# Two batches in nine-token rows: q, k and v loaded by head halves, kv in two row parts, the first factor by Sqrt, the last columns at full width

## The chip, the core and the metric

The kernel runs on one core of a Trainium2 chip. Its engines are TensorE (PE, matrix products), VectorE (DVE), ScalarE (ACT), GpSimd (POOL) and SyncE (SP, which here only issues transfers). Each has an instruction stream of its own; they meet through semaphores. The metric is the device time of one execution in microseconds (us), lower is better. The times given are medians over runs.

## The reference

q, k and v are fp32 arrays of 8 batches x 8 heads x 576 tokens x 64. An attention without softmax feeds a gated feed-forward layer:

```python
kv  = einsum('bhsd,bhse->bhde', k, v)                 # 64x64 for each batch and head
out = einsum('bhsd,bhde->bhse', q, kv)
out = out / sqrt(mean(out*out, -1) + 1e-6) * g_norm   # per head
x   = out.transpose(0, 2, 1, 3).reshape(4608, 512)    # heads side by side
xn  = x / sqrt(mean(x*x, -1) + 1e-6) * rms_g
y   = (silu(xn @ w_gate) * (xn @ w_val)) @ w_out      # 512 -> 1536 -> 512, fp32 out
```

## The kernel before

**Tiling.** The feed-forward layer makes nine groups of 512 tokens: one for each batch (its first 512 rows) and a ninth, `xr`, that gathers the 64 remaining rows of all eight batches. A group's x is held with features on partitions, in four feature blocks of 128. For each of 12 hidden blocks j, `slots_a` makes a gate product (four matmuls in `mm1`, L609, then Silu on ACT, L620) and a val product (four more, then the product `h` on VectorE, L626). `slots_b` multiplies h by w_out (`mm2`, L631) for each of four token tiles; ACT copies the tile to `osb` (L647) and SP's queue stores it (L649). Batch 0 uses `slots_b_by_j` instead, in which all four output tiles are open at once and their four stores come together at the end.

**Attention.** In a 512-row main part, row p*4+c sits on partition p, chunk c (NC = 4 chunks); the last 64 rows (`rem`) are loaded apart. `kv_mm` forms kv for two heads at once in a 128x128 product (L269), of which only the two diagonal 64x64 blocks are copied out; batch 1 uses 64-wide pieces instead (L263), and batch 0 `kv_pairs` (L281), two head pairs at a time. q is transposed on PE in batches 0 and 1 (`qT_mm`, L301, copied out at L311), by transfers on SP's queue in the others (`qT_dma`, L315 and L317). `o_mm` and `o_pairs` form q kv. The norms need two sums over each head, of out squared and of out squared times g_norm squared. Batches 0 and 1 get them from PE: `oT_mm` forms out transposed, ACT squares it (`sqT_`, L370), a matmul by the selector `sel` sums it (L378, L388). Later batches square on ACT (`sq_`, L348), multiply on GpSimd (`wsq`, L394) and sum on VectorE (`red`, L399). `chain` (L416 to L434) turns both sums into one factor `al`, by twelve small VectorE instructions that end in two Newton steps of 1/sqrt; `xna_` or `xna_pairs` (L444, L341) multiplies. x is then transposed by PE in batches 0 and 1 (`xT_mm`, L465, copied by ACT at L475 and by VectorE at L477, which also apply `gain`), by transfers on SP's queue in the others (`x_dma`, L496).

**Order.** Everything is issued in program order, by hand. Ahead of the loop, batch 0's first two chunks go through the whole attention while spins (`spin`, L227: matmuls on a tile of zeros) occupy PE. k and q arrive in fp32 through SP's and ACT's queues (`load_main`, L174) and are cast (L196); v arrives through GpSimd's queue, whose transfers cast to bf16 (`load_v01`). Then come 24 slots (`early`): gate and val of all 12 hidden blocks on the first 256 tokens; behind them `behind(n)` carries on with batch 0's other two chunks. From there a `Placer` takes over: it holds all later slots in order, knows how much time each engine has to spare in each kind of slot (`ROOM`) and how far it may fall behind (`BEHIND`), and puts the attention of the next batches between them. `place_second` places batch 1 by fixed slots, `place_attention` the others. `place_casts` puts the casts of staged q, k, v on GpSimd. `load_all(b)` issues a batch's loads on SP's queue while the batch two before it is in its feed-forward part: `load_all(3)` is placed six slots into batch 1, behind batch 2's `qT_dma`. Some loads carry an added wait (`add_manual_dep`) on an earlier transfer: batch 1's q on the last gate weights, batch 2's on the last of w_out.

`rows_of` gives the rows to which an output tile is stored: one store of 128 rows, or two of 64 in the group of the remaining rows.

Of the kernel before, what the change touches and what calls it, by code (L numbers as in the profile page):

```python
# [86 lines left out]
def kernel(  # L87
# [23 lines left out]
    FB0 = [sum(FB[:n]) for n in range(len(FB))]  # L111
    where = [(n, j - FB0[n]) for n in range(len(FB)) for j in range(FB0[n], FB0[n] + FB[n])]
# [28 lines left out]
    v01 = consts.tile([128, H, (NC + 1) * D], BF16, name="v01")  # L141
    k1 = consts.tile([128, H, (NC + 1) * D], BF16, name="k1")
# [11 lines left out]
    for t in range(2):  # L154
        nc.vector.memset(rems[t][0][REM:], 0.0)
    nc.vector.memset(v01[REM:, :, MAIN // 128 * D :], 0.0)
    idle = consts.tile([128, MAIN], BF16, name="idle")
    nc.vector.memset(idle, 0.0)
    nc.vector.memset(kvs[0], 0.0)
    nc.vector.memset(sel, 0.0)  # L160
    for half in range(2):
        nc.vector.memset(sel[half * D : (half + 1) * D, 0, half : half + 1], 1.0)

# [5 lines left out]
    def load_main(b, t, heads=(0, H), cs=(0, NC), queue=nc.sync):  # L169
        if (b, t) not in staged:  # L170
            staged[b, t] = stage.tile([128, H, NC * D], FP32, name="stg")
        h0, h1 = heads
        view = src[t][b, :, 0:MAIN, :].rearrange("h (p c) d -> p h (c d)", c=NC)
        return queue.dma_start(  # L174
            out=staged[b, t][:, h0:h1, cs[0] * D : cs[1] * D], in_=view[:, h0:h1, cs[0] * D : cs[1] * D]
        )

    def load_v01(b, heads=None, t=2):
        to = v01 if t == 2 else k1
        if heads is None:  # L180
            return nc.gpsimd.dma_start(
                out=to[:REM, :, NC * D :], in_=src[t][b, :, MAIN:S, :].rearrange("h p d -> p h d")
            )
        view = src[t][b, :, 0:MAIN, :].rearrange("h (p c) d -> p h (c d)", c=NC)[:, heads[0] : heads[1]]
        return nc.gpsimd.dma_start(out=to[:, heads[0] : heads[1], : NC * D], in_=view)
# [5 lines left out]
    def cast_main(b, t, eng, heads=(0, H), cs=(0, NC)):  # L191
        if (b, t) not in mains:
            mains[b, t] = qkv.tile([128, NC, H, D], BF16, name=f"main_{'qkv'[t]}")
        h0, h1 = heads
        copy = eng.copy if eng is nc.scalar else eng.tensor_copy
        return copy(  # L196
            out=mains[b, t][:, cs[0] : cs[1], h0:h1, :],
            in_=staged[b, t].rearrange("p h (c d) -> p c h d", c=NC)[:, cs[0] : cs[1], h0:h1, :],
        )
# [32 lines left out]
    class Att:  # L232
# [17 lines left out]
        def pair(self, t, c, j):  # L250
            if self.b < 2 and t == 2:
                return v01[:, 2 * j : 2 * j + 2, c * D : (c + 1) * D]
            return self.chunk(t, c)[:, 2 * j : 2 * j + 2, :]

        def kv_mm(self, js):
# [3 lines left out]
            for h in range(2 * js[0], 2 * js[-1] + 2) if self.b == 1 else ():  # L259
                rows, at = slice(h % 2 * D, h % 2 * D + D), slice(h % 2 * D, h % 2 * D + D)  # L260
                for c in self.kv_chunks:
                    cols = slice(c * D, (c + 1) * D)
                    nc.tensor.matmul(  # L263
                        self.kv_ps[rows, h // 2, at], lhsT=k1[:, h, cols], rhs=v01[:, h, cols],
                        start=c == 0, stop=c == NC, skip_group_check=True,
                    )
            for j in js if self.b > 1 else ():
# [7 lines left out]
        def kv_pairs(self, js, wait=0):  # L275
            ps = mm1_p.tile([128, 4, 2 * D], FP32, name="mm1")
            spin(flat(ps), wait)
            ps = ps[:, : len(js)]
            for i, j in enumerate(js):
                for c in self.kv_chunks:  # L280
                    nc.tensor.matmul(  # L281
                        ps[:, i, :], lhsT=self.pair(1, c, j), rhs=self.pair(2, c, j),
                        start=i == 0 and c == 0, stop=i == len(js) - 1 and c == NC, skip_group_check=True,
                    )
            return ps

        def kv_pairs_out(self, ps, js, half, eng):
            rows, cols = slice(half * D, (half + 1) * D), slice(half * D, (half + 1) * D)
            copy = eng.copy if eng is nc.scalar else eng.tensor_copy
            copy(out=self.kv[rows, js[0] : js[-1] + 1, half, :], in_=ps[rows, :, cols])  # L290
# [6 lines left out]
        def qT_mm(self, js, chunks, pool=None):  # L297
            qT_ps = (pool or att_p).tile([128, len(js), len(chunks) * 128], BF16, name="o2" if pool else "att")
            for n, j in enumerate(js):
                for i, c in enumerate(chunks):  # L300
                    nc.tensor.matmul(  # L301
                        qT_ps[:, n, i * 128 : (i + 1) * 128], lhsT=self.pair(0, c, j), rhs=ident, is_transpose=True,
                        start=True, stop=True, skip_group_check=True,
                    )
            return qT_ps

        def qT_out(self, ps, js, c0, eng):
            copy = eng.copy if eng is nc.scalar else eng.tensor_copy
            n = ps.shape[2] // 128
            to = self.qTj[:, js[0] : js[-1] + 1, c0 : c0 + n, :]  # L310
            copy(out=to, in_=ps.rearrange("p j (c t) -> p j c t", t=128))  # L311
# [60 lines left out]
        def stat_pairs(self, js, c0, c1, pool, name):  # L372
            first = self.st is None
            if first:
                self.st = pool.tile([128, 2, NC + 1, H], FP32, name=name)
            for c in range(c0, c1):
# [24 lines left out]
        def chain(self, c0, c1):  # L401

            if not hasattr(self, "al"):
# [3 lines left out]
                self.y = t("y", I32)  # L407
            cs = slice(c0, c1)
# [62 lines left out]
        def xT_out(self, j, chunks, eng):  # L471
            copy = eng.copy if eng is nc.scalar else eng.tensor_copy
            if self.b < 2 and chunks[0] < NC:
                if eng is nc.scalar:
                    copy = lambda out, in_: eng.mul(out=out, in_=in_, mul=gain[:, j : j + 1])  # L475
                else:
                    copy = lambda out, in_: eng.tensor_scalar(  # L477
                        out=out, in0=in_, scalar1=gain[:, j : j + 1], scalar2=None, op0=OP.mult
                    )
# [6 lines left out]
            else:  # L486
                copy(out=xr[:, j, self.b * REM : (self.b + 1) * REM], in_=xT)
# [63 lines left out]
    def place_second(P, s):  # L551
# [8 lines left out]
        dve(-1, 0.7, lambda: cast_main(1, 0, V, H0))  # L560
        act(-1, 1.04, lambda: cast_main(1, 0, A, H1))
        for j in range(NS):
            pe(j // 2, 0.23, ("q", j), lambda j=j: a.qT_mm((j,), range(NC)))
        P.at("PE", 1.14, lambda: a.kv_mm(range(NS)), s)
        dve(1, 0.42, lambda: a.qT_out(ps["q", 0], (0,), 0, V))
        act(1, 0.58, lambda: a.qT_out(ps["q", 1], (1,), 0, A))
        dve(1, 0.43, lambda: a.kv_out(0, V))
        dve(2, 0.43, lambda: a.kv_out(1, V))
        dve(2, 0.42, lambda: a.qT_out(ps["q", 2], (2,), 0, V))
        act(2, 0.58, lambda: a.qT_out(ps["q", 3], (3,), 0, A))  # L570
        act(2, 0.62, lambda: cast_rem(1, 0, A))
        pe(3, 0.23, ("q", NC), lambda: a.qT_mm(ALL, (NC,)))
        act(4, 0.58, lambda: a.qT_out(ps["q", NC], ALL, NC, A))
# [3 lines left out]
        o = lambda n: P.at("PE", 0.24, lambda: a.o_mm(n), s + (3, 4, 5, 5, 6)[n])  # L577
        for f, n in ((oT, 0), (o, 0), (oT, 1), (o, 1), (oT, 2), (o, 2), (oT, 3), (o, 3), (oT, 4), (o, 4)):
            f(n)
        for n in range(NC + 1):  # L580
            act((4, 5, 5, 6, 7)[n], 0.62, lambda n=n: a.sqT_(ps["oT", n], *parts[n]))
            dve((4, 5, 6, 6, 7)[n], 0.69, lambda n=n: a.outa_(n, V))
# [16 lines left out]
    def x_of(g, s, c0, c1):  # L599
# [3 lines left out]
        return xs[g][:, s, cs, :] if g < 2 else xs[g][:, cs, s, :]  # L603
# [31 lines left out]
    def rows_of(g, t):  # L635

        if g < B:
            view = out[g * S : g * S + MAIN, :].rearrange("(p c) d -> p c d", c=NC)
            return [(slice(0, 128), view[:, t, :])]
        return [  # L640
            (slice(n * REM, (n + 1) * REM), out[b * S + MAIN : (b + 1) * S, :])
# [86 lines left out]
    A.preload_act_table(ACT.Silu)  # L728
# [3 lines left out]

    for hsx, queue in ((H0, nc.sync), (H1, A)):
        rest = load_main(0, 0, hsx, cs=(2, 4), queue=queue)
        tc.add_manual_dep(rest.ins, v_loads[0].ins.name, SYNC, reason="k and v have the queues first")
    load_rem(0, 0)
# [4 lines left out]
    for t in range(3):  # L741
        for n in range(2):
            if n or t == 2:
                G.memset(rems[t][n][REM:], 0.0)
    G.memset(kvs[1], 0.0)
# [176 lines left out]
```

## Time and profile before

| | |
|---|---|
| median of 3 runs | 332.13 us (331.58 to 332.35) |
| span of the profiled execution, first to last instruction | 328.5 us |
| instructions | 5202 |
| TensorE | 315.4 us busy (96%), granted clock 1.000 |
| VectorE, ScalarE, GpSimd | 178.0, 142.3 and 99.3 us busy |
| up to the first gate matmul | 19.64 us, of which TensorE 13.57 busy |
| batch 0's remaining work, 19.64 to 60.30 | 40.66 us, TensorE 40.09 busy |
| batch 1's, 60.30 to 95.75 | 35.45 us, TensorE 34.10 busy |
| all later groups, 95.75 to 324.45 | 228.70 us, TensorE 227.69 busy |
| after the last matmul | 4.05 us |
| transfers | 48.15 MB, mean 147 GB/s |

How to read the lines that follow. One execution was profiled, and all durations are from it. The page gives the busy time of each engine (PEld is the loading of weights into TensorE, which overlaps its matmuls); "x1899" is a number of instructions; the digit rows cut the span into 40 slices, with the share in tenths. The chain of waits is the chain of work that ended last, in order of time: start, length, engine, what. DMA is a transfer; SPq, ACTq and POOLq are the parts of an engine that issue transfers. The timeline gives start, length, engine, line, operation, output<-input and, in brackets, idle time before it with what ended it. L12 is line 12 of the kernel's file. "128*64" behind MATMUL is the part of the array that it uses.

### The profile page before, as it was taken

Reading aid. Unit: us, or ns where it says so; the run is one execution under the profiler, and the core shown is the slowest. Engines: PE = TensorE matmul, PEld = TensorE weight load, DVE = VectorE, ACT = ScalarE, POOL = GpSimd, SP = SyncE. Lnnn points to the kernel's source line nnn. Section 1 sums busy time; section 2 is a strip of 40 time slices with the busy share of each in tenths; the row PEclk is TensorE's granted clock in tenths of the full one; section 3 lists DMA queues with packets and bytes.
Section 4 is the critical chain, followed back from the end, with each engine's and each line's share of the span. In section 5 each row is a group of like instructions: output and inputs, shape, how many; then the busy total and the mean of one; then the engine's idle time right before and its main releaser. Section 6 shows DMA issues by size and latency. Waiting matters only on the chain.

```text
span 328.5 us, 5202 instructions
## 1 busy us (share of the span) xinstructions
PE 315.4 (96%) x1899; PEld 164.8 (50%) x1919; DVE 178.0 (54%) x398; ACT 142.3 (43%) x268; POOL 99.3 (30%) x119
## 2 busy tenths in 40 slices
PE   7689999999999999999999999999999999999994
PEld 3368875454445445544554455444544444444442
DVE  3447467568958680768077807780678133203311
ACT  1375561568648422742274227422742233223320
POOL 8633010639506900690069005900420000000000
PEclk9999999999999999999999999999999999999999
DMA  8999999989279626981599079906000600020014
GB/s 206 223 201 203 232 167 306 274 266 255 71 182 346 138 35 168 317 188 24 159 305 215 14 163 299 229 9 168 34 1 0 170 32 0 32 98 0 0 34 97
DMA packets 78741, 48.15 MB, mean 147 GB/s; under 512 B 42744, under 2 KB 74236, under 8 KB 78716
## 3 DMA queue, kind: packets, MB, share of 16 engines
q1 hardware_dynamic: 66432, 40.41, 45.7%
q0 software_dynamic: 10544, 6.49, 13.5%
q10 hardware_dynamic: 1740, 0.92, 0.9%
q8 instruction: 15, 0.25, 0.3%
q14 instruction: 10, 0.08, 0.1%
HBM read 37.78 MB, written 9.44 MB: 144 GB/s over the span
## 4 chain that ended last, share of the span: by engine, by line
PE 84%; DMA 7%; DVE 4%; ACT 1%; issue 1%; POOL 1%; DVEq 0%; POOLq 0%; ACTq 0%
PE mm L609 53%; PE o L631 23%; DMA stg<-in_q_dram 4%; PE att L322 2%; DMA v<-in_v_dram 2%; PE att L269 2%; PE mm L631 1%; DMA x<-xna 1%; DVE h L626 1%; DVE xna L444 1%; PE o L660 1%; DVE wg L752 1%; PE att L301 1%; ACT x L475 1%; POOL main_q L196 0%
## 5 line engine op out<-in xcount | busy, mean ns | idle before, releaser
L626 DVE TENSOR_TENSOR h<-silu,mm 128x512 bf16<-128x512 bf16 (+1 forms) x120 | 75.7, 631 | 83.5 <-PE mm L609 71.8
L620 ACT ACTIVATE silu<-mm 128x512 bf16<-128x512 f32 (+1 forms) x120 | 66.6, 555 | 88.3 <-PE mm L609 79.0
L609 PE MATMUL mm<-x,wg 128*128 128x512 bf16 (+1 forms) x431 | 100.7, 355 | 1.2 <-DMA x<-xna 0.6
L609 PE MATMUL mm<-x,wv 128*128 128x512 bf16 (+1 forms) x430 | 100.3, 355 | 0.6 <-ACT osb L647 0.5
L631 PE MATMUL o<-wo,h 128*128 128x512 bf16 x383 | 87.4, 379 | 0.6
L609 PEld LDWEIGHTS <-wg 128*128 128x128 bf16 x480 | 46.4, 98 | 47.0 <-DMA x<-xna 1.1
L609 PEld LDWEIGHTS <-wv 128*128 128x128 bf16 x480 | 45.7, 98 | 41.6 <-issue 0.6
L631 PEld LDWEIGHTS <-h 128*128 128x128 bf16 x420 | 40.6, 98 | 46.7
L394 POOL TENSOR_TENSOR sq<-sq,g 128x512 bf16<-128x512 bf16 x30 | 34.2, 1152 | 95.7 <-ACT sq L348 95.7
L647 ACT COPY osb<-o 128x512 f32<-128x512 f32 x33 | 19.2, 587 | 67.7 <-PE o L631 67.7
L399 DVE TENSOR_REDUCE st<-sq 128x8 f32<-128x512 bf16 x60 | 38.3, 677 | 0.5 <-POOL sq L394 0.4
L295 DVE CAST kvs<-att 64x256 bf16<-64x256 f32 x14 | 5.9, 422 | 36.9 <-PE att L269 36.2
L444 DVE TENSOR_TENSOR xna<-outa,al 128x512 bf16<-128x512 bf16 x35 | 21.9, 682 | 0.1
L196 POOL CAST main_q<-stg 128x1024 bf16<-128x1024 f32 x12 | 12.6, 1058 | 20.6 <-ACT x L475 15.2
L348 ACT ACTIVATE sq<-att 128x512 bf16<-128x512 f32 x30 | 18.2, 606 | 0.5 <-PE att L322 0.5
L352 ACT CAST outa<-att 128x512 bf16<-128x512 f32 x30 | 17.8, 593 | 0.0
L322 PEld LDWEIGHTS <-qTs 128*128 128x128 bf16 x140 | 9.8, 98 | 5.2 <-issue 0.2
L609 PE MATMUL mm<-xr,wv 128*128 128x512 bf16 x47 | 12.3, 379 | 0.1
L609 PE MATMUL mm<-xr,wg 128*128 128x512 bf16 x47 | 12.3, 379 | 0.1
L196 POOL CAST main_k<-stg 128x1024 bf16<-128x1024 f32 x12 | 12.2, 1038 | 0.0
L196 POOL CAST main_v<-stg 128x1024 bf16<-128x1024 f32 x12 | 12.1, 1038 | 0.0
L322 PE MATMUL att<-kvs,qTs 128*128 128x128 bf16 x140 | 11.7, 219 | 0.0
(117 smaller groups left out, 183.4 us busy)
## 6 DMA issues: line engine op xcount, KB each, us to landing
out_dram<-osb SPq DMA_DIRECT2D x32, 256.0 KB, 2.5
stg<-in_q_dram SPq DMA_DIRECT2D x7, 1024.0 KB, 6.9
stg<-in_k_dram SPq DMA_DIRECT2D x6, 1024.0 KB, 9.2
stg<-in_v_dram SPq DMA_DIRECT2D x6, 1024.0 KB, 11.8
wg<-in_moe_w_gate_dram POOLq DMA_DIRECT2D x4, 384.0 KB, 15.7
wv<-in_moe_w_val_dram POOLq DMA_DIRECT2D x4, 384.0 KB, 17.1
wo<-in_moe_w_out_dram POOLq DMA_DIRECT2D x4, 384.0 KB, 18.2
stg<-in_k_dram SPq DMA_DIRECT2D x2, 512.0 KB, 6.2
```

The costliest lines, as they stand in the source:

```text
L196: return copy(out=mains[b, t][:, cs[0] : cs[1], h0:h1, :], in_=staged[b, t].rearrange("p h (c d) -> p c h d", c=NC)[:, cs[0] : cs[1], h0:h ...
L322: nc.tensor.matmul(o[:, 2 * j : 2 * j + 2, :], lhsT=self.qTj[:, j, c, :], rhs=self.kv[:, j, :, :], start=j == 0, stop=j == NS - 1, skip_gr ...
L348: nc.scalar.activation(out=self.sq[c][:, 0], in_=self.o[c], func=ACT.Square)
L352: (eng.tensor_copy if eng else nc.scalar.copy)(out=self.outa[c], in_=self.o[c])
L394: eng.tensor_tensor(out=self.sq[c][:, 1], in0=self.sq[c][:, 0], in1=g2, op=OP.mult)
L399: nc.vector.reduce_sum(out=self.st[:, which, c, :], in_=self.sq[c][:, which], axis=AX.X)
L444: return eng.tensor_tensor(out=self.xna[:, c], in0=src, in1=self.al[:, c, :].to_broadcast([128, H, D]), op=OP.mult)
L609: nc.tensor.matmul(ps[:, : c1 - c0], lhsT=w[n][:, s, jj * 128 : (jj + 1) * 128], rhs=x_of(g, s, c0, c1), start=s == 0, stop=s == NS - 1)
L620: nc.scalar.activation(out=si, in_=g_ps, func=ACT.Silu)
L626: nc.vector.tensor_tensor(out=hs[g, j][:, c0:c1], in0=box["silu"], in1=v_ps, op=OP.mult)
L631: nc.tensor.matmul(ps, lhsT=hs[g, j][:, t * 128 : (t + 1) * 128], rhs=wo[j // OB][:, j % OB, :], start=j == 0, stop=j == NF - 1)
L647: (eng.copy if eng is nc.scalar else eng.tensor_copy)(out=o, in_=ps)
```

## The change

Only batches 0 and 1 are laid out anew; what it does to the rest follows from the order.

- **Loads.** q, k and v of the two batches are split by heads: heads 0 to 3 on partitions 0 to 63, heads 4 to 7 on 64 to 127. Each partition holds nine successive tokens of a head (576 = 64 x 9), so nothing remains over, and the separate loads of `rem` go. v comes through GpSimd's casting queue as before, now in head-half pieces; k and q go by halves through SP's and ACT's queues (batch 1: all on SP's). Of batch 0's q four of nine columns (LEAD) are loaded first, the other five later, behind the third piece of v, and cast by GpSimd. Batch 1's k is no longer loaded by the casting queue but staged and cast by GpSimd; its loads wait on the third block of val weights instead of the last block of gate weights, and are issued at early slot 8 instead of 12.
- **kv.** `kv_half` issues 36 matmuls of 64 rows, alternately in the upper and the lower row half of the array, into two PSUM tiles; `kv_half_out` copies the diagonal blocks, the first tile's on VectorE, the second's on ACT. Before: 20 matmuls of 128 rows in batch 0, 40 pieces in batch 1.
- **First factor.** `lead_chain` replaces the first call of `chain`: a matmul puts the epsilon into PSUM ahead of the sums, then reciprocal, product, sum and a combined add and product on VectorE, Sqrt on ACT, a reciprocal on VectorE. ACT's table for Sqrt is loaded at the start, Silu's behind that Sqrt.
- **Order.** x's blocks of the two batches are kept in the order PERM = (0, 2, 1, 3), which follows from the head halves. The first nine hidden blocks (EARLY) of batch 0 run at half width as before, the last three at full width. The steps in `behind` move up: chain(2, 5) takes 7 slots instead of 8, xna and xT come earlier, and x's last chunk moves into the placer's first slots. `place_second` begins at slot EARLY + 3. The memset of the tile that the spins read comes first; the last spins are 5 instead of 6.
- **Stores.** A tile of batches 0 and 1 now holds two tokens for each of 64 partitions' rows, so that `rows_of` gives two stores of 64 rows for each of their tiles.

```diff
+    NT = S // D
+    LEAD = 4
+    PERM = (0, 2, 1, 3)
+    EARLY = 9
...
+    def load_half(b, t, hh, queue, hl=(0, 4), cs=(0, NT)):
...
+        view = src[t][b].rearrange("(g h) (p c) d -> g p h (c d)", g=2, c=NT)[hh]
+        hs, xs = slice(*hl), slice(cs[0] * D, cs[1] * D)
+        return queue.dma_start(out=to[hh * 64 : hh * 64 + 64, hs, xs], in_=view[:, hs, xs])
...
     def load_all(b):
         if b == 1:
-            first = load_main(b, 0)
-            load_rem(b, 0)
-            return first
+            return [load_half(b, t, hh, nc.sync) for t in (1, 0) for hh in range(2)][0]
...
+        def kv_half(self, jjs, pool, name, wait=0):
+
+            k_, v_ = mains[self.b, 1], mains[self.b, 2]
+            ps = [pool.tile([128, 4, 2 * D], FP32, name=name) for _ in range(2)]
+            spin(flat(ps[0]), wait)
+            for n, jj in enumerate(jjs):
+                for c in range(NT):
+                    for hh in range(2):
+                        rows = slice(hh * 64, hh * 64 + 64)
+                        nc.tensor.matmul(
+                            ps[hh][:, n, :], lhsT=k_[rows, c, 2 * jj : 2 * jj + 2, :],
+                            rhs=v_[rows, 2 * jj : 2 * jj + 2, c * D : (c + 1) * D],
+                            start=c == 0, stop=c == NT - 1, skip_group_check=True,
+                        )
             return ps
...
+                if guard:
+                    nc.tensor.matmul(
+                        self.st[:, 0, c0:c1, :], lhsT=ones, rhs=epsr[:, : (c1 - c0) * H], start=True, stop=True,
+                        skip_group_check=True,
+                    )
+                    first = False
...
+        def lead_chain(self, c0, c1):
...
+            V.reciprocal(out=r, in_=u)
+            V.tensor_tensor(out=t, in0=self.st[:, 1, cs], in1=r, op=OP.mult)
+            V.reduce_sum(out=s, in_=t, axis=AX.X)
+            V.scalar_tensor_tensor(
+                out=z, in0=s.to_broadcast([128, w, H]), scalar=H * eps, in1=u, op0=OP.add, op1=OP.mult
+            )
+            nc.scalar.activation(out=nt, in_=z, func=ACT.Sqrt)
+            nc.scalar.preload_act_table(ACT.Silu)
+            V.reciprocal(out=al, in_=nt)
...
     def rows_of(g, t):
 
+        if g < 2:
+            view = out[g * S : (g + 1) * S, :].rearrange("(p c) d -> p c d", c=NT)
+            return [(slice(n * 64, n * 64 + 64), view[:, 2 * t + n, :]) for n in range(2)]
...
-    v_loads = [load_v01(0, hsx) for hsx in (None, H0, H1)]
-    load_main(0, 1, H0)
-    load_main(0, 0, cs=(0, 2), queue=A)
-    load_rem(0, 1)
-    load_main(0, 1, H1)
-    A.preload_act_table(ACT.Silu)
+    v_loads = [load_half(0, 2, hh, G, (2 * jj, 2 * jj + 2)) for jj in range(2) for hh in range(2)]
+    for t, cs in ((1, (0, NT)), (0, (0, LEAD))):
+        for hh, queue in ((0, nc.sync), (1, A)):
+            load_half(0, t, hh, queue, cs=cs)
...
+    A.preload_act_table(ACT.Sqrt)
+    late = [load_half(0, 0, hh, nc.sync, cs=(LEAD, NT)) for hh in range(2)]
+    tc.add_manual_dep(late[0].ins, v_loads[2].ins.name, SYNC, reason="k and v have the queues first")
...
-    cast_main(0, 0, V, cs=(0, 2))
-    cast_main(0, 1, V, H0)
-    cast_rem(0, 1, V)
-    for js, eng in ((P0, A), (P1, V)):
-        a.qT_out(a.qT_mm(js, (0, 1)), js, 0, eng)
-    kva = a.kv_pairs(P0, 4)
-    cast_main(0, 1, A, H1)
-    a.kv_pairs_out(kva, P0, 0, V)
-    a.kv_pairs_out(kva, P0, 1, V)
-    ta = a.oT_mm(P0, 0, 2, o2_p, 3)
-    a.sqT_(ta, P0, 0, 2)
-    kvb = a.kv_pairs(P1)
+    cast_half(0, 1, V, (0, 2))
+    cast_half(0, 0, A, cs=(0, 2))
+    cast_half(0, 0, V, cs=(2, LEAD))
+    cast_half(0, 1, A, (2, 4))
+    for jj, eng in ((0, V), (1, A)):
+        a.qT_out(a.qT_mm((jj,), lead), jj, 0, lead, eng)
+    kva = a.kv_half((0,), mm1_p, "mm1", 4)
+    for hh, eng in ((0, V), (1, A)):
+        for half in range(2):
+            a.kv_half_out(kva, (0,), hh, half, eng)
+    ta = a.oT_mm(P0, 0, chunks, o2_p, 3)
+    a.sqT_(ta, P0, 0, chunks)
+    kvb = a.kv_half((1,), att_p, "att")
...
-    early = [s for j in range(NF) for s in slots_a(0, j, 0, half)]
+    early = [s for j in range(EARLY) for s in slots_a(0, j, 0, half)]
...
-        if n == 12:
+        if n == 8:
             gate = load_all(1)
-            tc.add_manual_dep(gate.ins, w_loads[-1][0].ins.name, SYNC, reason="the weights come first")
+            tc.add_manual_dep(gate.ins, w_loads[2][1].ins.name, SYNC, reason="the weights come first")
...
-    slots = [one(slots_a(0, j, half, MAIN)) for j in range(NF)] + slots_b_by_j(0)
+    slots = [one(slots_a(0, j, half, MAIN)) for j in range(EARLY)]
+    slots += [s for j in range(EARLY, NF) for s in slots_a(0, j)] + slots_b_by_j(0)
...
-            end = place_second(P, 9)
+            end = place_second(P, EARLY + 3)
```

More of the change, by code (lines that the diff above doesn't have):

```diff
@@ L159 @@
     nc.vector.memset(kvs[0], 0.0)
+    for n in range(2):
+        pad = qTs[n].rearrange("p c j t -> p (c j t)").rearrange("p (j t) -> p j t", j=NS)[:, :, S:]
+        nc.vector.memset(pad, 0.0)
     nc.vector.memset(sel, 0.0)
@@ L162 @@
         nc.vector.memset(sel[half * D : (half + 1) * D, 0, half : half + 1], 1.0)
+    nc.vector.memset(ones, 1.0)
+    nc.vector.memset(epsr, D * eps)
     src = (q, k, v)
@@ L258, in kv_mm @@
                 self.kv_n = 0
[L259 to L267, printed above, removed]
+            for j in js:
                 for c in self.kv_chunks:
@@ L273, in kv_mm, with kv_half_out @@
                     self.kv_n += 1
[L275 to L284, printed above, removed]
+        def kv_half(self, jjs, pool, name, wait=0):
[11 more added lines that the diff above has]
+                        )
             return ps
-        def kv_pairs_out(self, ps, js, half, eng):
+        def kv_half_out(self, ps, jjs, hh, half, eng):
             rows, cols = slice(half * D, (half + 1) * D), slice(half * D, (half + 1) * D)
             copy = eng.copy if eng is nc.scalar else eng.tensor_copy
-            copy(out=self.kv[rows, js[0] : js[-1] + 1, half, :], in_=ps[rows, :, cols])
+            to = self.kv.rearrange("p (j h) t d -> p j h t d", h=2)[rows, jjs[0] : jjs[-1] + 1, hh, half, :]
+            copy(out=to, in_=ps[hh][rows, : len(jjs), cols])
         def kv_out(self, half, eng):
@@ L486, in xT_out @@
             else:
-                copy(out=xr[:, j, self.b * REM : (self.b + 1) * REM], in_=xT)
+                to = PERM[j] if self.b < 2 else j
+                copy(out=xr[:, to, self.b * REM : (self.b + 1) * REM], in_=xT)
         def x_dma(self, c0, c1):
@@ L740 @@
     w_loads = [load_w(n) for n in range(len(FB))]
[L741 to L745, printed above, removed]
-    G.memset(k1[REM:, :, NC * D :], 0.0)
     def fold(w, s, eng):
@@ L855 @@
         behind(n)
+    for jj in range(2):
+        cast_half(1, 1, G, (2 * jj, 2 * jj + 2))
     gsq = consts.tile([128, D], FP32, name="gsq")
@@ L871 @@
     P = Placer(slots, 3)
+    P.at("PE", 0.15, lambda: a.xT_mm(ALL, (NC,)), 0)
+    P.at("ACT", 1.2, lambda: [a.xT_out(j, (NC,), A) for j in ALL], 1)
     casts = ()
```

212 lines of the change are left out of this document (108 added, 104 removed).

## The prediction

> **What bounds the kernel now.** I read the page first, for the bound; then the chain of waits, for the places where something other than TensorE decides; then the timeline of those places, engine by engine.
>
> ```profile
> span 328.5 us, 5202 instructions
> PE 315.4 (96%) x1899; PEld 164.8 (50%) x1919; DVE 178.0 (54%) x398; ACT 142.3 (43%) x268; POOL 99.3 (30%) x119
> PEclk9999999999999999999999999999999999999999
> ```
>
> PE is busy 96% of the span at full granted clock. Stages split at chosen times show what is not PE-bound: 19.64 us before the first gate matmul (its 13.6 us of PE are mostly spins), 1.35 us idle in 60.30:95.75, 4.05 us after the last matmul, and about 1.6 us elsewhere. An edit pays only if it shortens the lead-in, removes PE work behind it, or moves one of those waits. The chain of waits (start, length, what):
>
> ```profile
> 7.42 8.34 DMA stg<-in_q_dram
> ...
> 18.85 0.24 PE mm L465 x4
> 19.11 0.85 ACT x L475 x2
> ...
> 67.02 6.01 DMA stg<-in_q_dram
> ...
> 73.17 0.47 POOL main_q L196
> ...
> 75.19 1.12 POOL sq L394
> 76.34 0.81 DVE st L399 x2
> ...
> 92.52 3.18 DMA x<-xna
> 95.75 1.04 PE mm L609 x4
> ```
>
> Two stretches count. The first is the lead-in. The second starts in SP's queue: the load of batch 3's q is issued at 67.02, GpSimd waits for it, its two casts stand ahead of batch 2's sq products (L394), VectorE's sums (L399) wait for those, and the chain, xna and x transposes that follow are so late that PE idles before 95.75. What stands before 67.02 on SP:
>
> ```profile
> 60.97 1.83 SPq L649 DMA_DIRECT2D out_dram<-osb  x4
> 62.98 2.65 SPq L315 DMA_TRANSPOSE qTs<-main_q  x1
> 65.75 1.18 SPq L317 DMA_TRANSPOSE qTs<-remq  x1
> 67.02 0.54 SPq L174 DMA_DIRECT2D stg<-in_q_dram  x1
> ```
>
> Batch 0's four stores come straight before the transposes and that load. Last, single rows that price the edits:
>
> ```profile
> 1.28 1.28 ACT L728 ACT_TABLE_LOAD   x1 [1.28 <-PEq L906]
> 14.88 0.17 DVE L416 TENSOR_SCALAR u<-mm 128x16 f32<-128x16 f32 x1 [0.60 <-PE mm L378]
> 17.26 0.17 DVE L434 SCALAR_TENSOR_TENSOR al<-nt,al 128x16 f32<-128x16 f32 x1
> 29.58 0.40 PE L465 MATMUL o<-ident,xna 128*128 128x128 bf16 x4 [0.32 <-DVE xna L341]
> 43.07 0.88 PE L263 MATMUL att<-v,k 128*64 128x64 bf16 x40
> ```
>
> **Lead-in, loads.** Before, 2.36 MB (k, its rest, first q chunks, half of v with its rest) had landed by 10.4 us, at 260 GB/s in 2.1:10.4 (a casting load counts its halved output). After, k 1.18, q's four lead columns 0.52 and the first half of v 0.59 MB are needed: 2.29 MB, the same. Rows become 2304 bytes instead of 256 to 1024; at the rate of the bulk loads (338 GB/s in 50:60) it would be done near 8.5, at the old rate near 10. q's lead comes last on its queues, so the first cast of q, which ran at 6.45, waits; I take 9.0 (8.5 to 9.8).
>
> **Lead-in, compute, from q at 9.0.** ACT casts 512 columns (0.61, as L203): 9.7. Eight transposes (0.45), four spins (0.86), then kv. L269's ten 128-wide matmuls take 0.56, so 0.056 each; 18 with 64 rows take 0.5 if two row halves overlap, 1.0 if not. In the trace L263's 64-column pieces ran 40 in 0.81, 0.020 each where a 64-wide matmul alone would need some 0.027; tiles overlapped there, so I take 0.5: 11.5 against 11.12. kv leaves in four 64x64 copies on two engines (about 0.45, from 0.59 for two 64x128): 12.2 against 11.80, +0.4. The second kv half leaves on both engines, -0.2. The chain took twelve VectorE ops, 14.88 to 17.43 = 2.55; now five (two reciprocals 0.25, three at 0.17, 0.04 between) plus one Sqrt on ACT, which no row shows: 0.25 estimated from ACT's small ops and 0.2 for two handovers, 1.6 in all, -0.95 (bounds -1.3 to 0). The late q transposes no longer stand ahead of xT, and x is consumed in PERM order, ACT and DVE by turns: -0.3. Sum -1.05 at the end of the first gate (20.44 before); bounds -1.8 to +0.5.
>
> The second table load falls behind Sqrt, beside the last reciprocal (0.25), xna (0.65) and xT (0.46), 1.36 in all: at the row's 1.28 it costs nothing. [...]
>
> **From there to batch 1's first gate (60.30).** Ten transposes follow the first gate instead of four: 6 x 0.056 = +0.33. ACT cannot use the whole head start: silu, then the copies and squares that ran 20.53 to 23.35 gain a small copy (about 0.25) and a wait for PE (about 0.3), so some 0.4 of it reaches VectorE's second chain. That chain is spread over seven slots, not eight, so one h product (0.42) fewer stands inside: xT at 29.58 comes about 0.85 earlier, of which 0.1 is work moved behind it. Batch 1's kv: 18 pairs x 0.056 = 1.0 against 0.81, its q two transposes fewer, three full-width columns save 24 x 0.005: together +0.3 or so. Stage sum: batch 1 starts 0.4 earlier (bounds -1.0 to +1.0). Covers for the rest: GpSimd's cast of late q (1.04 x 1.25 = 1.3) must end by 19.4; its load is released by v's third piece, near 9.3, and earlier gated loads issued at 7.4 landed at 15.8, so about 17.1 plus 1.3 = 18.4, 1 us of slack. Batch 1's q must land by about 41; it is released two weight blocks earlier (third wv against last wg, 26.5 against 28.4) but carries twice the bytes, and lands near 40 (39.8 before). If either cover fails, PE stalls for the rest, up to 1 us.
>
> **SP's queue.** Each of batch 0's four output tiles now leaves in two 64-row stores. The trace's six 64-row stores took 0.47 to 0.59 each to issue, the 128-row ones 0.36 to 0.53; back to back the four at 60.97 step by 0.49. Four more: 1.5 (0.37 each) to 2.5 (0.59 plus the gaps), I take 2.0. Queued behind them: the q transposes of batch 2, then q of batch 3, for which GpSimd waits. L315's issue took 1.66 to 5.52 over six; with batch 2's loads long done it might fall from 2.65 toward 1.66, so between 0.5 and 2.5 reaches the load: 1.7. VectorE has 0.16 to spare (its idle before h at 84.33), hence +1.5 at 95.75. The rest of SP's extra work is covered: batch 1's extra stores delay q of batch 4 by about 1.1, against 1.7 between sq's end (105.3) and the sum that reads it (107.0).
>
> **Sum.** -0.4 + 1.5 = +1.1. The profiled execution's span goes from 328.5 to 329.6. The median, 332.13, lies 3.6 above that span; this remainder and the 4.05 us tail stay. Forecast 333.2. About 0.2%, 0.66 us, can be told from no change here.
>
> **Rivals.** (1) SP's extra stores hide. In SP's own list of waits one L315 stands with 2.5 us on a GpSimd cast (remk, done at 65.43); if SP was held until then anyway, two microseconds of stores cost 0.5 or less. Against it: that instruction's start, not its end, follows its named waits elsewhere (L317 starts as remq's cast ends). Then -0.4 + 0.2, or with more of the head start kept -0.9: 331.2 to 331.9, 331.5. This is the faster side; it decides if q of batch 3 is issued no more than 0.3 us later after batch 1's first gate than before (6.72). (2) The row halves run one after the other: 0.5 more in each lead-in part and 1.0 more in batch 1, of which ACT's own limit hides some: 334.5. For it: no row here has 64-row matmuls. (3) The clock falls back. The spins end earlier (idle's memset is first now, spins from about 1.2 to 6.7) and PE then waits for q: 9.7 less 6.7 = 3.0 us, against at most 1.9 before. The first seven spins ran at 0.43 instead of 0.216 for about 3 us; if that returns, transposes, spins and kv double, +2: 335.2. [...]
>
> **Chances.** Forecast case 0.44, its own range 332.5 to 334.2; of it 0.10 is within 0.2%. Rival 1 0.28, of which 0.06 within. Rivals 2 to 4: 0.14, 0.07, 0.07, all slower. So faster 0.22, same 0.16, slower 0.62. The range 331.1 to 335.0 leaves out about 0.1 at each end.
>
> **What would show it.** In the changed kernel's profile: Sqrt between VectorE's two reciprocals, the first gate ending near 19.4; row-half matmuls in pairs with half the step; batch 1's first gate 0.4 earlier; eight stores before L330, q of batch 3 landing about 1.7 later against batch 1's first gate, and more PE idle before batch 2's first gate. I am wrong if that gate shows no added wait, or if the lead-in ends later than 20.4.

## The result, and the profile after

The changed kernel takes 340.28 us (339.93 to 341.18, 4 runs) beside 331.89 for the one before: a ratio of 1.027, interval 1.0238 to 1.0301. That is 8.4 slower where 1.1 was forecast, outside the range. The profiled spans differ by 9.6, more than the medians: over all comparisons before's executions took about 330.4 where their mean granted clock was 0.996 or more, as in the profiled one, and about 331.8 where it was lower, and a span is some 1.8 shorter than the time. Stages are compared in the profiles, totals in the medians.

The page of the changed kernel, three lines:

```profile
span 338.1 us, 5194 instructions
PE 320.6 (95%) x1904; PEld 163.4 (48%) x1904; DVE 175.7 (52%) x391; ACT 142.2 (42%) x268; POOL 101.8 (30%) x122
PEclk9699999999999999999999999999999999999998
```

PE's busy time grew by 5.2. The clock dips in the second slice (and in the last, behind PE's last matmul). Its stages, cut at the first gate matmuls of batches 0, 1 and 2 (start:end, length, busy time of PE, PEld, DVE, ACT, POOL, granted clock, DMA share, GB/s):

```profile
0.00:24.66 24.66, 16.30 (x109) 7.80 (x110) 6.72 (x27) 7.59 (x14) 12.53 (x24) 0.86 1.08 204
24.66:66.72 42.06, 41.12 (x390) 28.78 (x389) 26.72 (x72) 20.21 (x48) 10.64 (x17) 1.00 1.00 220
66.72:105.35 38.63, 34.58 (x200) 16.96 (x198) 24.83 (x60) 23.14 (x44) 19.61 (x22) 1.00 0.79 179
```

| stage | before | changed | difference |
|---|---|---|---|
| lead-in | 19.64 | 24.66 | +5.02 |
| batch 0 | 40.66 | 42.06 | +1.40 |
| batch 1 | 35.45 | 38.63 | +3.18 |
| batch 2 | 33.33 | 33.50 | +0.17 |

Everything later is equal to 0.02 a batch. The chain of waits of the changed kernel (start, length, what):

```profile
12.26 15.31 DMA wv<-in_moe_w_val_dram
...
29.55 17.88 DMA stg<-in_q_dram
...
48.40 0.62 PE att L314 x8
...
76.56 5.91 DMA stg<-in_q_dram
...
86.99 0.69 DVE h L666
...
87.72 1.04 PE mm L649 x4
...
101.98 3.32 DMA x<-xna
```

Up to 48.40 the chain holds no compute of batch 0 at all: batch 1's q, released by the third block of val weights, lands at 47.42, and batch 1's transposes wait for it. Behind that, batch 3's q (76.56) again makes a block's h late, and then batch 2's x. In the lead-in's timeline (start, length, what):

```profile
9.23 0.83 DVE L217 CAST main_k<-stg 128x1152 bf16<-128x1152 f32 x1 [7.06 <-DMA stg<-in_k_dram]
...
12.43 0.62 ACT L217 CAST main_q<-stg 128x512 bf16<-128x512 f32 x1 [7.47 <-DMA stg<-in_q_dram]
...
13.93 1.91 PE L245 MATMUL mm<-idle 128*128 128x512 bf16 x4
...
22.34 0.21 ACT L441 ACTIVATE nt<-z 128x16 f32<-128x16 f32 x1 [1.25 <-DVE z L438]
22.58 1.28 ACT L442 ACT_TABLE_LOAD   x1
...
24.13 0.84 ACT L516 ACTIVATE x<-mm,gain 128x256 bf16<-128x256 bf16 x2 [0.27 <-PE mm L505]
```

k is cast at 9.23 and q only at 12.43; PE had been idle since 7.1, and its next four spins took 1.91 where 0.86 was expected: the granted clock was 0.50 from 11.74 to 18.57. The first gate matmuls ended at 25.66, later than the 20.4 that the prediction gave as a sign of being wrong. SP's queue behind batch 1's first gate (66.72):

```profile
67.39 5.03 SPq L693 DMA_DIRECT2D out_dram<-osb  x8
...
76.56 0.53 SPq L177 DMA_DIRECT2D stg<-in_q_dram  x1
```

Eight stores hold SP for 5.03 where four held it for 1.83, and batch 3's q is issued 9.84 behind batch 1's first gate instead of 6.72.

### The profile page after: what moved, and what is told of

Read it like the earlier page. It is cut to its first block, busy times and chain, and to the rows that moved or that the text cites. A ratio compares the mean times of both kernels' runs of the same rounds, so it can differ in the third digit from the quotient of the medians.

```text
span 338.1 us, 5194 instructions
## 1 busy us (share of the span) xinstructions
PE 320.6 (95%) x1904; PEld 163.4 (48%) x1904; DVE 175.7 (52%) x391; ACT 142.2 (42%) x268; POOL 101.8 (30%) x122
## 4 chain that ended last, share of the span: by engine, by line
PE 72%; DMA 15%; DVE 4%; POOL 3%; issue 2%; SPq 2%; ACT 1%; POOLq 0%; DVEq 0%; ACTq 0%
PE mm L649 44%; PE o L671 22%; DMA stg<-in_q_dram 7%; DMA wv<-in_moe_w_val_dram 5%; DMA main_v<-in_v_dram 3%; PE att L337 2%; PE att L277 1%; PE mm L671 1%; DMA x<-xna 1%; DVE h L666 1%; DVE xna L484 1%; DVE st L420 1%; POOL main_q L205 1%; DVE wg L785 1%; POOL main_k L205 1%
## 5 line engine op out<-in xcount | busy, mean ns | idle before, releaser
L671 PE MATMUL o<-wo,h 128*128 128x512 bf16 x396 | 89.9, 379 | 0.0
L649 PEld LDWEIGHTS <-wg 128*128 128x128 bf16 x468 | 45.2, 98 | 51.1 <-issue 4.1
L649 PEld LDWEIGHTS <-wv 128*128 128x128 bf16 x468 | 44.5, 98 | 42.7 <-issue 0.8
L308 DVE CAST kvs<-att 64x256 bf16<-64x256 f32 x12 | 5.1, 421 | 36.5 <-PE att L277 36.4
```

Of the source, the lines that this page charges most:

```text
L649: nc.tensor.matmul(ps[:, : c1 - c0], lhsT=w[n][:, s, jj * 128 : (jj + 1) * 128], rhs=x_of(g, s, c0, c1), start=s == 0, stop=s == NS - 1)
L671: nc.tensor.matmul(ps, lhsT=hs[g, j][:, t * 128 : (t + 1) * 128], rhs=wo[j // OB][:, j % OB, :], start=j == 0, stop=j == NF - 1)
```

## The experiments

**Does the late lead-in cost anything, and is it the idle clock?** `spins`: it runs 44 first spins instead of 18.

```diff
-    spin(mm1_p.tile([128, MAIN], FP32, name="mm1"), 18)
+    spin(mm1_p.tile([128, MAIN], FP32, name="mm1"), 44)
```

> The changed kernel with 44 spins instead of 18 at the start, so that PE is busy until q is cast (about 12.7 instead of 7.1, first transpose at 13.1). Theory (clock falls back): the four later spins ran at 0.43 instead of 0.216 us and eight transposes took 1.04 instead of 0.45, because PE had been idle for 6.2 us; with the spins they run at full rate, the first gate comes at about 23.0 instead of 24.66. But the time hardly moves, within 0.5 of 340.3: batch 1's q lands at 47.42, whatever PE does, so the wait before its transposes at 48.40 grows from 0.26 to about 1.8. Rival (head start kept): 338.6. Rival (the slow rate has another cause than the idle time): first gate as it was, 24.6.

It takes 340.56 (ratio to before 1.0287). In the profile the granted clock was 1.000 from 4.87 on, and the first gate came at 22.18, 2.48 earlier; but batch 1's first gate came at 66.68, only 0.04 earlier. So filling the idle time took the clock's fall away, and the time didn't change. Two waits of PE took the head start back, for the cast of late q and for batch 1's q:

```profile
24.14 0.73 PE L314 MATMUL att<-ident,main_q 128*128 128x128 bf16 x10 [0.95 <-POOL main_q L217]
...
48.36 0.62 PE L314 MATMUL att<-ident,main_q 128*128 128x128 bf16 x8 [1.45 <-DVE main_q L217]
```

**Why are the loads late?** Three variants of batch 0's k and q loads. `rows` cuts k's rows in two (1024 and 1280 bytes). `both` lets each transfer fill both partition halves, with the half as its outer dimension of size 2. `full128` spreads each transfer over 128 uniform partitions.

```diff
# rows
+    for t, cs in ((1, (0, LEAD)), (1, (LEAD, NT)), (0, (0, LEAD))):
...
# both (one head of each half at a time)
+        view = src[t][b].rearrange("(g h) (p c) d -> h g p (c d)", g=2, c=NT)[h]
...
# full128 (two heads of each half at a time)
+        view = src[t][b].rearrange("(h g) (p c) d -> (g p) h (c d)", g=2, c=NT)
...
```

> The changed kernel with each half of k loaded in two transfers, four and five columns wide (rows of 1024 and 1280 bytes instead of 2304), still to 64 partitions each. Theory (64 partitions are slow): the bytes move at the same 200 GB/s (a 1024-byte packet takes about 80 ns), q's lead lands within 0.7 of 12.35. Rival (long rows are slow): packets of 1024 bytes take 46 to 59 ns as before the change, q's lead lands near 9.5.

It took 341.23 in its one execution; q was cast at 12.87, and the first gate came at 24.05. Short rows change nothing: while one half of k moved without the other, 1280-byte packets took mostly 92 to 111 ns. From 7.5 on, with the other half's packets of q beside them, they took 68.

> The changed kernel with batch 0's k and lead columns of q loaded by one head of each half at a time, over all 128 partitions (SP: head offsets 0 and 1, ACT: 2 and 3), rows of 2304 and 1024 bytes as in the change, the same bytes on the same queues. Theory (64 partitions are slow): in the changed kernel a 2304-byte packet took 170 to 190 ns (16 engines: 200 GB/s) where k went to 64 partitions at a time; over 128 partitions it takes about 110 (335 GB/s, the rate of 1024-byte rows before), k has landed near 6.5 instead of 9.1, q's lead near 9 instead of 12.35, PE's gap falls under 3 us, the first gate comes near 20.5. Rival (long rows are slow): packets still take 170 to 190 ns, q lands near 12. Rival (the order alone: q stands behind all of k): q lands where k's rate puts it, no change. If the lead-in gains 4 us, batch 1's q, released by the weights that land behind these loads, decides what is kept: 336.5 to 339.

It takes 384.48, with the first gate at 69.39. This tested something else: SP's and ACT's queues each moved only some 18 KB per us, eight packets. But those 2304-byte packets, to both halves, mostly took 93 to 106 ns. Eight packets of about 0.1 us in each us keep less than one DMA engine busy: up to 13 us SP's queue filled 5.7% of the time of 16 engines, ACT's 2.8%. What held the queues back was not shown.

> The changed kernel with batch 0's k and lead columns of q loaded to all 128 partitions by each transfer (SP heads 0 to 3, ACT 4 to 7, even heads to the lower half and odd ones to the upper), rows of 2304 and 1024 bytes and the number of bytes and queues as in the change. Their heads then stand in other places than v's, so it forms products of the wrong heads, of the same sizes. Theory (a transfer to 64 partitions that runs alone is slow: 2304-byte packets took 170 to 200 ns while ACT's half, then SP's, ran alone, and 93 to 106 where one such packet ran alone on its engine): packets take about 105, k has landed near 6, q's lead near 9 instead of 12.35, PE's gap falls from 6.2 to about 3, the first gate comes near 20.5. Rival (2304-byte rows are slow whatever the partitions): packets at 170 or more, q near 12, first gate within 0.7 of 24.66. The time stays within 1 of 340.3 in both cases, since batch 1's q lands late whatever the lead-in does; it may come earlier by as much as the weights do, up to 2.

It takes 338.64, with the first gate at 18.80. From issue to landing, the changed kernel's loads of k and q, then full128's (KB each, us):

```profile
stg<-in_k_dram ACTq DMA_DIRECT2D x1, 576.0 KB, 5.5
stg<-in_k_dram SPq DMA_DIRECT2D x1, 576.0 KB, 8.4
...
stg<-in_q_dram ACTq DMA_DIRECT2D x1, 256.0 KB, 10.8
```

```profile
stg<-in_k_dram ACTq DMA_DIRECT2D x1, 576.0 KB, 5.4
stg<-in_k_dram SPq DMA_DIRECT2D x1, 576.0 KB, 5.0
...
stg<-in_q_dram ACTq DMA_DIRECT2D x1, 256.0 KB, 7.8
```

In the changed kernel ACT's half of k ran first (packets from 2.27 to 5.12) and SP's after it (4.71 to 8.01). Each moved 205 to 219 GB/s. SP's packets mostly took 155 to 200 ns; ACT's took mostly 93 up to 4.0 and mostly 181 to 194 from then on. Spread over 128 partitions, nearly all of the same packets took 93, both queues at once, 383 to 407 GB/s. Bytes, row lengths and queues are the same, so the destination's partitions make the difference. How they make it was not shown, and the prediction did not count on it. Batch 1's first gate still came at 63.49, behind an idle time of 0.92 for batch 1's q, whose loads were halves still.

**Is batch 1's q late only because it is released late?** `early_b1`: the spins, and the second val block as the gate.

```diff
-            tc.add_manual_dep(gate.ins, w_loads[2][1].ins.name, SYNC, reason="the weights come first")
+            tc.add_manual_dep(gate.ins, w_loads[1][1].ins.name, SYNC, reason="the weights come first")
```

> The changed kernel with 44 spins at the start (first gate at 22.2 as with the spins alone) and with batch 1's k and q released by the second block of val weights (landed at 22.7) instead of the third (27.6). Theory (batch 1's q is the wall behind batch 0): q lands 2 to 5 earlier than 47.42, the transposes of batch 1 come as much earlier, at most 2.3, and so does batch 1's first gate (64.4 to 65.5 instead of 66.7): 338 to 339.5. Rival (the queues are full until then, so that an earlier release only takes from the weights): batch 1's first gate within 0.5 of 66.7, and waits for weights in batch 0's gates and vals.

It takes 338.69, 1.6 less than the changed kernel. In the profile the wait for batch 1's q is gone, but PE's clock fell back at 23.74, in the wait for late q, so that batch 1's first gate, 66.25, hardly shows it:

```profile
22.00:26.00 4.00, 3.08 (x23) 2.25 (x24) 1.26 (x4) 1.93 (x5) 3.23 (x5) 0.72 1.31 203
26.00:30.00 4.00, 4.00 (x44) 3.43 (x43) 1.31 (x4) 2.30 (x6) 3.33 (x6) 0.86 1.24 245
```

The last weights landed at 40.0 instead of 31.4, as the rival said they might. The profiled execution, 340.87, was the slowest of the four; the others, with a mean clock of 1.000, took 336.73 to 338.94. So this stays inconclusive; the next one decides.

**All loads at full width.** `full_ok` spreads every load of batches 0 and 1 over 128 partitions. Even and odd heads then share a transfer, so the strided columns of q kv and of the sums put the heads back in order.

```diff
-    PERM = (0, 2, 1, 3)
+    PERM = (0, 1, 2, 3)
...
-        view = src[t][b].rearrange("(g h) (p c) d -> g p h (c d)", g=2, c=NT)[hh]
+        view = src[t][b].rearrange("(h g) (p c) d -> (g p) h (c d)", g=2, c=NT)
...
+        def hs(self, j):
+            return slice(4 * (j // 2) + j % 2, 4 * (j // 2) + 4, 2) if self.b < 2 else slice(2 * j, 2 * j + 2)
...
-                    o[:, 2 * j : 2 * j + 2, :], lhsT=self.qTj[:, j, c, :], rhs=self.kv[:, j, :, :],
+                    o[:, self.hs(j), :], lhsT=self.qTj[:, j, c, :], rhs=self.kv[:, j, :, :],
...
```

> The changed kernel with every load of q, k and v of batches 0 and 1 spread over all 128 partitions (even heads on the lower half, odd on the upper, two heads of each half per transfer), and the heads put back into their order where TensorE writes q kv and the sums (strided columns), so that x is in feature order; bytes, row lengths, number of transfers and stores as in the change. Theory (transfers to 64 partitions cost both the lead-in and batch 1's q): first gate near 18.8 as with batch 0's k and q alone, batch 1's q lands at 42 or earlier instead of 47.42 and the wait before its transposes is under 0.3, batch 1's first gate at 60 to 61 instead of 66.7; its stage stays at 38 to 39 because of the eight stores: 333.5 to 335. Rival (batch 1's q is late because it is released late and the queues are full): batch 1's first gate as with batch 0's loads alone, 63.5 or later: 337 or more.

It takes 334.41 (1.0106, 1.0069 to 1.0142). Lead-in and batch 0:

```profile
0.00:18.76 18.76, 13.86 (x108) 6.73 (x109) 6.78 (x27) 7.48 (x14) 10.19 (x21) 1.00 1.06 232
18.76:60.60 41.84, 41.07 (x390) 28.69 (x389) 26.45 (x72) 20.20 (x48) 12.79 (x20) 1.00 1.06 237
```

Batch 1's q was cast at 41.40 without a wait; its first gate came at 60.60, against 66.72 and, before the change, 60.30. The half-partition loads are worth 1.0270 less 1.0106, or 5.4 us. Batch 1's stage, with its eight stores, stays long: 38.53.

**The stores.** `one_store` was to undo them, `b_stores` doubles them in the kernel before, `q3_early` loads batch 3's q ahead of them.

```diff
# one_store
+            return [(slice(0, 128), view[:, 2 * t : 2 * t + 2, :].rearrange("p n d -> n p d"))]
# b_stores
+            parts = [slice(n * 64, n * 64 + 64) for n in range(2)] if g < 2 else [slice(0, 128)]
+            return [(rows, view[rows, t, :]) for rows in parts]
# q3_early
+        first = [load_main(b, t) for t in ((1, 2) if b == 3 else (0, 1, 2))][0]
+    P.at("SP", 0.0, lambda: load_main(3, 0), EARLY + 4)
```

> The changed kernel, with each output tile of batches 0 and 1 stored by one 128-row transfer again (both tokens of a row in one access pattern) instead of two of 64 rows. Theory (SP's queue): in the changed kernel the eight stores took 5.03 us of SP against 1.83 for four before, and batch 3's q was issued 9.84 after batch 1's first gate instead of 6.72. With four stores it is issued about 6.7 to 7.2 after it, VectorE's 3.44 idle before its sums falls to under 0.5, PE's 2.42 idle in batch 1 goes, and batch 1's stage falls from 38.6 to about 35.6: 337.2 against 340.3 in time. Rival (GpSimd's casts): the transposes of batch 2's q end with GpSimd's cast of remv (ends 73.13), whatever stands ahead of them on SP; then q of batch 3 moves by less than 0.5 and the time by less than 0.5.

It takes 369.8 and undoes nothing. Its outer dimension is 2 again; four stores held SP for 10.07, the transposes of main q behind them 13.06. So it decides nothing between its theory and its rival.

> The kernel before, with each output tile of batches 0 and 1 stored in two transfers of 64 rows instead of one of 128; nothing else. Theory (SP's queue): the eight stores take about 5.0 of SP, as in the changed kernel, instead of 1.83; batch 3's q is issued about 9.9 after batch 1's first gate instead of 6.7; batch 1's stage, 35.45, becomes about 38.5, and all else stays: 332.1 + 3 = 335. Rival (the transposes of batch 2's q wait for GpSimd's casts anyway): issued by 7.5 at the latest, under 0.8 slower.

It takes 333.21 beside 331.34 (1.0071, 1.0038 to 1.0104), which is 1.9 slower by the medians and 2.4 by the ratio. SP:

```profile
62.56 5.02 SPq L650 DMA_DIRECT2D out_dram<-osb  x8
67.76 1.79 SPq L315 DMA_TRANSPOSE qTs<-main_q  x1
...
70.93 0.54 SPq L174 DMA_DIRECT2D stg<-in_q_dram  x1
```

Each of these 64-row stores takes 0.54 to 0.59 to issue, each of the four 128-row ones before 0.36 to 0.38. The main transposes gave 0.86 back (1.79 for 2.65), and q was issued 9.04 behind batch 1's first gate (61.89); batch 1's stage grew by 2.19. (The profiled lead-in, 21.23, is longer for another reason: the granted clock was 0.85 on average from 10.00 to there, before any store.)

> The changed kernel with the load of batch 3's q issued on SP behind batch 2's loads, ahead of batch 0's eight stores and of the transposes of batch 2's q; its other loads stay. Theory (GpSimd waits for that load, behind the stores): the load lands near 67, GpSimd casts it without waiting, VectorE's idle of 3.44 before its sums goes, PE's 2.42 and most of the 1.43 before batch 2's first gate with it; batch 1's stage falls from 38.6 to about 35.3: 337. Rival (the late sums have another cause, late squares on ACT or late q transposes behind the eight stores): the stage falls by less than 1.5.

It takes 337.16, 3.1 less than the changed kernel; batch 1's stage was 35.71. The rival falls.

**Both causes gone.** `full_q3` joins `full_ok` and `q3_early`.

> The kernel of full_ok, and batch 3's q loaded ahead of batch 0's stores as in q3_early. Theory (two causes, loads to 64 partitions and the eight stores, that add up): batch 1's stage 35.5 instead of 38.6, batch 2's first gate near 95.7 to 96.5, as before the change; 330.5 to 332, so that nothing is left of the change's loss. Rival (a third cause): more than 333.

It takes 331.10 beside 331.05 (1.0002, 0.9986 to 1.0018): by the medians nothing is left of the loss, and no gain stands behind it. The profiles, both at a granted clock of 1.000, still differ by 1.2: the lead-in is 0.83 shorter, the stages of batches 0, 1 and 2 are 1.17, 0.29 and 0.88 longer. The profiled execution was the slowest of its twelve, 0.5 above their median, so at an equal clock about 0.7 of a loss stays.

**What is left before batch 2's first gate.** `b_q3` loads batch 3's q early in the kernel before, with q3_early's edit.

> The kernel before with batch 3's q loaded ahead of batch 0's stores; nothing else. Theory (that load sets the 0.78 us of waiting before batch 2's first gate): the wait falls to under 0.2 and batch 1's stage from 35.45 to about 34.8: 0.5 to 0.8 faster than before. Rival (the sums and the chain behind them are late anyway): no change.

It takes 331.62 (0.9999): the theory fell. The transposes of batch 2's q, now beside that load, took 5.77 on SP instead of 2.65, and PE's wait stayed at 0.79. (Waits like this one are counted from the end of the last matmul's step of 0.216; the idle time of the views, 0.62 here as before, is some 0.16 shorter.) The chain of `full_q3` pointed elsewhere: eight foldings of gain into the gate weights stand among batch 2's chain and xna on VectorE. `full_best` (on `full_q3`, batch 4's q early as well) and `b_fold` (on the kernel before) put them later; `full_fold2` and `b_fold2` put all twelve right behind xna.

```diff
# full_best, b_fold
-            for n, at in ((0, 6), (1, 24), (2, 30), (3, 40)):
+            for n, at, dve_at in ((0, 6, 6), (1, 24, 36), (2, 30, 40), (3, 40, 44)):
...
# full_fold2, b_fold2 (blocks 1 to 3, VectorE's)
+                            P.at(eng, 0.0, do, starts[1] + 36 + n)
...
# full_best, full_fold2
+    P.at("SP", 0.0, lambda: load_main(4, 0), starts[1] + 12)
```

> The kernel of full_q3 with the foldings of gain into blocks 1 to 3 of the gate weights moved on VectorE behind batch 2's xna, and batch 4's q loaded 12 slots into batch 1 instead of at the start of batch 2. Theory (what is left of the waits is VectorE's folding, eight pieces of about 0.23 between the chain and the xna of batch 2, and the late q of batch 4): batch 2's xna ends about 1.8 earlier, the wait of 1.06 before its first gate goes, the one of 0.78 at 109.2 too: 329.0 to 329.8, 0.4 to 0.6% faster than before. Rival (the x transposes then wait for something else on SP): 330.5 to 331.

It takes 331.33 (1.0011, 0.9995 to 1.0027): batch 1's stage is 35.38 instead of 35.74, but batch 2's is 34.38 instead of 34.21.

> The kernel before with those foldings moved in the same way; nothing else. Theory (in the kernel before, too, the 0.78 us of waiting before batch 2's first gate comes from the foldings among chain and xna, not from batch 3's q, whose earlier load left it as it was): the wait goes, batch 1's stage falls from 35.45 to about 34.7, 0.7 faster. Rival (the wait is set by the x transposes on SP): no change.

It takes 330.39 (0.9991, 0.9975 to 1.0007): batch 1's stage is 35.09, batch 2's 33.67. Both theories were half right; what moved into batch 2 cost there what it saved.

> The kernel of full_best with the twelve foldings on VectorE all put right behind batch 2's xna, where it idled 4.4 us, instead of partly in batch 2. Theory (in full_best the foldings behind batch 2's start made its h late by 0.9, which gave back what batch 1's stage gained): batch 1's stage stays at 35.4, batch 2's falls from 34.4 to 33.4 to 33.8: 330.3, 0.1 to 0.3% faster than before. Rival (batch 4's q or GpSimd makes that h late): no change against full_best, 331.3.

It takes 330.31 (0.9990, 0.9972 to 1.0008): batch 2's stage is 33.32, near what was expected; a wait of 0.70 before its first gate stays. The time can't be told from that of the kernel before.

> The kernel before with those twelve foldings in the same place; nothing else. Theory: batch 1's stage 35.1 as with b_fold, batch 2's 33.3 instead of 33.67: 0.3 to 0.5 faster than before. Rival (the foldings were not what made batch 2 later): as b_fold, within 0.2% of before.

It takes 330.25 beside 331.07 (0.9976, 0.9959 to 0.9994), which is 0.24% faster than the kernel before and the only variant whose interval lies below it. Batch 1's stage is 34.76, batch 2's 33.33, and the wait of 0.78 is gone. VectorE there:

```profile
88.73 3.10 DVE L444 TENSOR_TENSOR xna<-outa,al 128x512 bf16<-128x512 bf16 x5
91.74 2.84 DVE L752 TENSOR_SCALAR wg<-wg,gain 128x384 bf16<-128x384 bf16 x12
```

Before, the five xna ran from 89.09 to 93.10 with foldings between them; now they end at 91.83.

## Why the prediction was wrong

- **Loads of the lead-in: the failed step.** "At the rate of the bulk loads it would be done near 8.5, at the old rate near 10": both rates were of transfers to 128 partitions. q landed at 12.35, not 9.0. With full-width loads its two halves landed at 8.92 and 9.10 in `full128`, and in `full_ok` the first gate came 0.88 earlier than before; the sum said 1.05.
- **The cover of batch 1's q: the second failed step.** It was to land "near 40", and if not, to cost "up to 1 us". It landed at 47.42, and batch 1's first gate came 6.4 later than before, where the forecast had it 0.4 earlier. The forecast counted the bytes at the old pace, though these were four half-partition transfers in one queue; at full width, `full_ok` had q cast from 41.40 on. The cover of late q failed too, once the lead-in was shortened: in `spins` PE was idle for 0.95.
- **SP's queue: right mechanism, term too small.** The stores took 3.2 longer, not 2.0: the sum priced four more stores, but all eight are 64-row stores now, and each costs more to issue than a 128-row one (0.54 to 0.60 against 0.36 to 0.38). 3.12 reached the load, not 1.7, because the transposes behind the stores gave back only 0.07 (3.88 for 3.95); batch 1's stage grew by 3.18, not 1.5. In `b_stores` they gave back 0.86. Why they did not in the changed kernel is open. That the change came out slower, as forecast, rests on this term alone; the larger loss, 5.4, stood in the sum as a gain of 0.4.
- **Before's wait of 0.78** was put down to batch 3's q. `b_q3` gained nothing by loading it earlier; the transposes beside it took 3.1 longer, so this doesn't clear that load. `b_fold2` took the wait away and left the load where it was, so VectorE's foldings held it.
- **Compute terms** held in the main. Sqrt took 0.21 (0.25 estimated) and the lead chain, 21.44 to 22.84, 1.40 (1.6). Batch 1's 36 matmuls of 64 rows took 1.11, 0.031 each against 0.056 with 128 rows; so the price of overlapping row halves held, and rival 2 falls. One term was too small: batch 0's stage grew by 1.18 with full-width loads, where the terms from there to batch 1 came to 0.65; PE's busy time in it grew by 0.98.
- **Rival 3**, the clock, happened behind a longer gap, 6.0, and cost nothing in time, by `spins`, since batch 1's q came later still.
- **Rival 4**, that the switch of ACT's table costs more than its load, is shown by no run. In the changed kernel the load began 0.03 behind the end of Sqrt and took 1.28, as in the row of the kernel before, and ACT's first x began 0.27 behind the end of the load, released by PE's transposes.
- **Rival 1** falls: the stores don't hide, by `b_stores` and `q3_early`.

## What to carry to other kernels

Price a transfer by a run that reaches the same partitions, not by bytes and row length alone: here the same rows moved at 205 to 219 GB/s to 64 partitions and at 383 to 407 to 128, and k's two halves on two queues ran mostly one after the other (packets from 2.27 to 5.12 and from 4.71 to 8.01), so that they didn't add up. The layout that splits partitions showed up again at the stores, as eight issues in 5.03 us instead of four in 1.83, on a queue where other work stands behind them. When a head start vanishes, look for the next wait that is tied to a transfer's release and not to the engine that was sped up (here batch 1's q, landed at 47.42).

## What had not been expected of the hardware

- PE's granted clock also fell to half for 3.4 us after an idle time of 2.26 us in `early_b1` (matmuls from 0.216 to 0.43) and of 2.35 us in `full128`, though 2.26 us in the changed kernel and 2.33 us in `spins` left it at full rate.
- In `both`, each queue moved only about 18 KB per us with transfers whose outer dimension is 2.
- k's two halves, issued at the same time on two queues, moved mostly one after the other (packets from 2.27 to 5.12 and from 4.71 to 8.01). Where packets for both halves did move side by side, as in `rows` from 7.5 on, they were no longer slow: 68 ns for 1280 bytes instead of 92 to 111.
